# A sparse-attention and mixture block on one Trainium2 core: zero fills on VectorE, later constants behind stage one, and all of batch 0's stage one ahead of the projection weights

## The chip, the cores and the metric

The kernel runs on one core of one Trainium2 chip. The metric is the device time of one execution in microseconds; lower is better. Before the change it is 478.81 us, the median of three runs (478.75, 478.81 and 481.27).

## What is computed

Inputs are q, k and v of 4 batches, 8 heads, 576 positions and 64 columns, and the weights of two blocks. Three steps follow one another:

```python
# stage one: attention with fixed masks; half the heads see the last 32 positions,
# half see every 32nd position before their own
mask_local = (rel >= 0) & (rel < stride)
mask_strided = (rel >= 0) & (pos[None, :] % stride == pos[:, None] % stride)
x = softmax(where(mask, scale * q @ k.T, -1e9)) @ v          # as (4, 576, 512)
# stage two: 4 experts of causal attention, each row takes the 2 of the largest gate
topk = np.argpartition(-(x @ w_gate), K, axis=-1)[..., :K]
out += mask * w * (softmax(causal(scale * q @ k.T)) @ v @ wo[e])
# stage three: h = relu(x @ w_in), a convolution of width 3 over positions, a gate
return (h * sigmoid(conv(h)) @ w_out).astype(np.float32)
```

w_in, conv_w and w_out come as 64-bit words, which the kernel turns into pairs of 32-bit parts on the chip.

## The kernel before

**Stage one** of a batch consists of four units: `s1_local(b, 0)`, `s1_local(b, 1)`, `s1_strided(b, 0)` and `s1_strided(b, 1)`. A unit loads its q and k into a buffer `un` (two exist), lays the mask into PSUM with a matmul of `m_sel` and a mask tile (line 222), adds the scores (line 226), copies them out on ScalarE into `sp` (local) or `pp` (strided), and runs the softmax (lines 229 to 243): maximum on VectorE, subtraction on GpSimd, exponential on ScalarE, sum and reciprocal on VectorE, product on GpSimd. VectorE transposes the result into `lp` (lines 309, 382), ScalarE and GpSimd spread it into the block-diagonal tile `bd` (line 249), and TensorE multiplies with v: `av` for local units (line 324), `avs` for strided ones (line 392). ScalarE and VectorE write the result as two half-precision parts `xt` (lines 252, 254). `sp`, `pp`, `bd`, `vn` and `vs` exist once each, so a unit follows another through them. `bd` must be zero outside its blocks; it is filled once at the start, as are the masks.

**Weights.** `w_proj(kk)`, four times, loads a block of the projection weights into a staging buffer `st` and splits it in two parts (`wvg` on ScalarE, `wqk` and the lower parts on VectorE, lines 722 to 725). `w_wp(hf, kk)`, eight times, loads a block of w_in into an `st` buffer, turns it into numbers (`f64_parts`, lines 697 to 705, over ScalarE, VectorE and GpSimd, with a scratch tile `fc`), and multiplies it with `wo` on TensorE: `wps` (line 750). There are two `st` buffers for all of these blocks. `w_wo` loads `woT`, `w_taps` the taps of the convolution, and `w_out_part` (called O below, tile `ow`) w_out, after the staging buffers have been released.

**Stage two** projects x: `p_v` (`psv`, lines 108 to 110 through line 425) and `p_qk` (`psq`), then per block of rows the attention unit `a_unit` with scores `asc`, mask `m_c`, probabilities `pn` (four zero-filled buffers) and result `zav`, written to `z` or, for the last rows, `zL`. The gate in `p_gate` uses the small constant `tri`. **Stage three** is `s3_step`: `hps`, taps on VectorE (line 637), and `o`.

**What sets the order.** Every piece is a generator; a string of letters (line 823) says in which order they are started and how many steps all live ones take after each: S for a stage-one unit, J for `w_proj`, W for the other weights, P for a projection, A for an attention unit, O and M as above. The framework then schedules what has been emitted, engine by engine, by a timeline of its own, so the rows of an engine do not stand in the order of the code. Each engine executes its own row in order. All loads are issued by SyncE's queue, also in order.

Of the kernel before, what the change touches and what calls it, by code (L numbers as in the profile page):

```python
# [7 lines left out]
F32 = mybir.dt.float32  # L8
F32R = mybir.dt.float32r
U32 = mybir.dt.uint32  # L10
F16 = mybir.dt.float16
BF16 = mybir.dt.bfloat16
ACTF = mybir.ActivationFunctionType
ALU = mybir.AluOpType
# [15 lines left out]
C2 = SM / (Q_S * Q_S)  # L30
# [7 lines left out]
NEG = -1.0e9  # L38
# [7 lines left out]
def moe_stack_kernel(ctx, tc, qk_in, vloc, vstr, w_p, wo_t, w_in, conv_w, w_out, out):  # L46
    nc = tc.nc
    B, S, _ = vstr.shape
    D = 64
    DM, DFF = w_in.shape  # L50
    E = wo_t.shape[1] // D
    KD = DM // 128
# [10 lines left out]
    const = pool("const", 1)  # L63
# [10 lines left out]
    act, dve, gp = nc.scalar, nc.vector, nc.gpsimd  # L74
# [20 lines left out]
    def copy_a(out, in_, scale=1.0):  # L95
        act.activation(out=out, in_=in_, func=ACTF.Copy, scale=scale)  # L96
# [29 lines left out]
    for rows, nb in ((first, 4), (extra, 1)):  # L126
        for sign in (1, -1):
            gp.affine_select(out=m_sel[rows, 0:nb], in_=m_sel[rows, 0:nb], pattern=[[0, nb], [sign, 32]],
                             compare_op=ALU.is_ge, fill=0.0, base=0, channel_multiplier=-sign)
    gp.affine_select(out=m_loc[first], in_=m_loc[first], pattern=[[0, NG + 1], [1, 64]],  # L130
                     compare_op=ALU.is_gt, fill=NEG / C1, base=0, channel_multiplier=-1)
    gp.affine_select(out=m_loc[first], in_=m_loc[first], pattern=[[0, NG + 1], [-1, 64]],
                     compare_op=ALU.is_ge, fill=NEG / C1, base=32, channel_multiplier=1)
    dve.memset(m_loc[extra, 0], -NEG / C1)
    gp.affine_select(out=m_loc[extra, 0], in_=m_loc[extra, 0], pattern=[[-1, 64]],
                     compare_op=ALU.is_ge, fill=NEG / C1, base=0, channel_multiplier=1)
    gp.affine_select(out=m_loc[extra, 0], in_=m_loc[extra, 0], pattern=[[-1, 64]],
                     compare_op=ALU.is_ge, fill=0.0, base=32, channel_multiplier=1)
    gp.affine_select(out=m_str[first], in_=m_str[first], pattern=[[0, 8], [-1, NPOS]], compare_op=ALU.is_ge,
                     fill=NEG / C1, base=0, channel_multiplier=1)  # L140
    for x in (m_sel, m_loc, m_str):
        dve.tensor_copy(out=x[64:128], in_=x[0:64])
    m_sel = m_sel.rearrange("p j i -> p (j i)")
    m_loc = m_loc.rearrange("p g c -> p (g c)")
    m_str = m_str.rearrange("p n c -> p (n c)")
# [13 lines left out]
    for x in free["vs"] + free["pp"]:  # L159
        dve.memset(x, 0.0)  # L160
    for _, x in free["bd"]:
        gp.memset(x, 0.0)

    def take(what):

# [3 lines left out]

    def give(what, x):  # L170
        free[what].append(x)

    m_c = const.tile([128, S], BF16, name="m_c")
    gp.memset(m_c, 0.0)
    gp.affine_select(out=m_c[:, S - 128:], in_=m_c[:, S - 128:], pattern=[[-1, 128]], compare_op=ALU.is_ge,
                     fill=NEG / C2, base=0, channel_multiplier=1)
    tri = const.tile([128, E, E], F32, name="tri")
    gp.memset(tri, 0.0)
    gp.affine_select(out=tri, in_=tri, pattern=[[1, E], [-1, E]], compare_op=ALU.is_gt,
                     fill=-1.0, base=0, channel_multiplier=0)  # L180
    gp.tensor_scalar(out=tri, in0=tri, scalar1=1.0, scalar2=None, op0=ALU.add)

    pn_free = []

# [495 lines left out]
            "h": pool("h", H_BUFS), "g": pool("g", G_BUFS), "pn": pool("pn", 1)}  # L680
    pn_free.extend(late["pn"].tile([128, 1280], F16, name=f"pn{i}") for i in range(4))
    zL = [late["zl"].tile([128, 2, 4, 66], F32R, name=f"zL{i}") for i in range(2)]
    for x in pn_free:
        gp.memset(x.bitcast(U32), 0)
    for x in zL:
        gp.memset(x.bitcast(F32), 0.0)
    wout = []
    stg = tc.alloc_tile_pool(name="stg", bufs=2)
    woT = stg.tile([128, KD, E * D], F32, tag="woT", bufs=1, name="woT")
# [41 lines left out]
    def w_wo():  # L731
        nc.sync.dma_start(out=woT, in_=wo_t.rearrange("(k p) n -> p k n", p=128))
        yield
# [3 lines left out]
    def w_wp(hf, kk):  # L737
        cs = slice(512 * hf, 512 * hf + 512)
        t = stg.tile([128, 512, 2], U32, tag="st", name="st")
        nc.sync.dma_start(out=t.rearrange("p n w -> p (n w)"), in_=w_in[128 * kk:128 * kk + 128, cs].bitcast(U32))  # L740
        wi = stg.tile([128, 512], F32, tag="wi", name="wi")
        fc = stg.tile([128, 512], F32, tag="fc", name="fc")
        yield
        a, f = f64_parts(t, fc)
        e2("wa").tensor_tensor(out=wi, in0=a, in1=f, op=ALU.add)
        yield
        if kk == 0:
            wps[hf] = [ps_o.tile([128, 512], F32, tag=f"o{r}", name="wps") for r in range(2)]
        for r in range(2):
            nc.tensor.matmul(out=wps[hf][r], lhsT=woT[:, kk, 128 * r:128 * r + 128], rhs=wi,  # L750
                             start=kk == 0, stop=kk == KD - 1)
        if kk == KD - 1:
            yield
            for r in range(2):
                copy_a(wp[0][:, r, cs], wps[hf][r])
                sub(dve, wp[1][:, r, cs], wps[hf][r], wp[0][:, r, cs].bitcast(F32))
            if hf == 1:
                done.add("wp")

    def w_taps():  # L760
        t = stg.tile([128, 1024], U32, tag="st", name="ct")[:, 0:2 * 3 * KF].rearrange("p (n w) -> p n w", w=2)
        nc.sync.dma_start(out=t.rearrange("p n w -> p (n w)"), in_=conv_w.bitcast(U32))
        yield
        a, f = f64_parts(t, taps)
        gp.tensor_tensor(out=taps, in0=a, in1=f, op=ALU.add)
        yield
        done.add("taps")
# [11 lines left out]
    def mix(*streams):  # L779

        at = [(((i + 0.5) / len(s), n, x)) for n, s in enumerate(streams) for i, x in enumerate(s)]
        return [x for _, _, x in sorted(at, key=lambda t: t[:2])]
# [21 lines left out]
    def rel():  # L804
# [8 lines left out]
        "S": [u for b in range(B) for u in s1_items(b)],  # L813
        "J": [w_proj(kk) for kk in range(KD)],
        "P": [u for b in range(B) for u in p_items(b)],
        "W": [w_wo()] + [w_wp(hf, kk) for hf in range(2) for kk in range(KD)] + [w_taps()],
        "A": [u for b in range(B) for u in a_items(b)],
        "O": [w_out_part(f, hf) for f in range(KF) for hf in range(2)],
        "M": [s3_step((b, ch), f) for b in range(B) for ch in range(2) for f in range(0, KF, 2)]
             + [s3_step(None, f) for f in range(0, KF, 2)],  # L820
    }
    streams = {k: iter(v) for k, v in streams.items()}
    order = list("SSJJJJSS") + mix("W" * 10, "P" * 13, "S" * 4) + ["R"]
    for b in range(B):
        m = "M" * (KF // 2 if b else 0)
        o = "O" * (8 if b == 0 else 0)
# [66 lines left out]
```

## Time and profile before

| | |
|---|---|
| profiled execution, its own time | 479.27 us |
| span of its trace | 477.6 us |
| median of three runs | 478.81 us |
| mean granted TensorE clock, share of full speed | 0.953 |
| TensorE matmuls busy | 407.0 us, 85% |
| VectorE busy | 343.6 us, 72% |
| ScalarE busy | 312.3 us, 65% |
| GpSimd busy | 182.5 us, 38% |

The trace is one execution. Times in its rows count from the start of the span. A row of the timeline gives the start, the time from first start to last end, the engine, the line, the operation, the tile written and those read (without buffer numbers), shape and type, how many instructions are merged in it, and in brackets the idle time of the engine before it with what ended it. A row of the windows gives start and end, length, the busy time of PE, PEld (its weight loads), DVE, ACT and POOL with their instructions, the granted clock, the busy share of the DMA engines and GB/s. A row of the waits says which engine and operation waited for which, for how long in total, how often, and the longest. PE is TensorE, DVE VectorE, ACT ScalarE, POOL GpSimd, SPq SyncE's queue of loads and stores. Several matmuls overlap, so a sum of their single durations is more than their busy time.

### The profile page before, as it was taken

The numbers are of one execution on the slowest core, as the hardware profiler recorded it, in microseconds if no ns is written. First come the engines' busy times: TensorE is split into PE (matmuls) and PEld (weight loads), VectorE is DVE, ScalarE is ACT, GpSimd is POOL, SyncE is SP. The second block draws the span as 40 slices with busy tenths as digits, with TensorE's granted clock in tenths as the row PEclk, the third lists the DMA queues.
The fourth block names the chain that finished last, engine by engine and source line by source line (L and its number), as shares of the span: only waits on it lengthen the run. The fifth ranks groups of instructions, "written<-read, shape, count | busy, mean of one in ns | idle before, by whom it ended". The sixth has DMA issues, their size and how long they took to land.

```text
span 477.6 us, 12531 instructions
## 1 busy us (share of the span) xinstructions
PE 407.0 (85%) x4736; PEld 296.3 (62%) x4736; DVE 343.6 (72%) x970; ACT 312.3 (65%) x833; POOL 182.5 (38%) x247
## 2 busy tenths in 40 slices
PE   0565869797677589999999899999999999999994
PEld 0352446565545467667777667767876677778873
DVE  4498776879979988987874795588757887465651
ACT  1172453568868747777982796698568997567662
POOL 8156656334654532643530243123212333233231
PEclk9995889999579879999999999999999999999999
DMA  5985574236695762253723044254313655101011
GB/s 151 262 266 163 117 224 133 73 112 134 130 181 153 178 140 73 55 112 75 133 44 71 1 102 82 23 117 86 60 51 56 104 104 99 45 1 44 1 46 44
DMA packets 105981, 48.31 MB, mean 101 GB/s; under 512 B 77504, under 2 KB 100032, under 8 KB 105920
## 3 DMA queue, kind: packets, MB, share of 16 engines
q1 hardware_dynamic: 105920, 47.50, 43.0%
q8 instruction: 37, 0.61, 0.5%
q14 instruction: 24, 0.20, 0.1%
HBM read 27.56 MB, written 4.72 MB: 68 GB/s over the span
## 4 chain that ended last, share of the span: by engine, by line
PE 52%; DVE 18%; DMA 13%; issue 5%; ACT 5%; SPq 4%; POOL 2%; POOLq 0%; ACTq 0%; DVEq 0%
PE o L109 7%; PE o L108 7%; PE o L110 6%; DMA st<-in_dram 5%; DMA apt<-pn 4%; PE zav L585 4%; PE asc L535 4%; PE hps L108 4%; DMA ow<-in_dram 3%; PE hps L109 3%; PE hps L110 2%; PE psq L108 2%; PE psq L110 2%; PE psq L109 2%; PE psv L108 2%
## 5 line engine op out<-in xcount | busy, mean ns | idle before, releaser
L637 DVE SCALAR_TENSOR_TENSOR t<-hs,taps,t 128x256 f32<-128x256 f32 x144 | 78.5, 548 | 33.1 <-ACT t L96 32.0
L105 POOL TENSOR_TENSOR gl<-t,gh 128x512 fp32r<-128x512 f32 x36 | 48.3, 1341 | 73.5 <-ACT gh L96 49.5
L109 PE MATMUL o<-wout,gl 128*128 128x512 f32 x144 | 59.1, 410 | 2.3 <-POOL gl L105 2.3
L110 PE MATMUL o<-wout,gh 128*128 128x512 f32 x144 | 56.7, 394 | 0.0
L108 PE MATMUL o<-wout,gh 128*128 128x512 f32 x144 | 55.2, 416 | 0.6 <-ACT gh L96 0.4
L105 POOL TENSOR_TENSOR pn<-apf,pn 64x64 f16<-64x64 f32 (+4 forms) x40 | 33.7, 846 | 51.7 <-ACT pn L96 38.9
L545 ACT ACTIVATE apf<-apf,anm 64x64 f32<-64x64 f32 (+4 forms) x80 | 44.6, 559 | 6.1 <-DVE anm L539 5.7
L585 PE MATMUL zav<-apt,v 128*64 128x128 f16 (+2 forms) x720 | 35.7, 224 | 11.1 <-DMA apt<-pn 4.6
L108 PE MATMUL hps<-z,wp 128*128 128x258 f32 x128 | 40.7, 318 | 2.4 <-ACT hs L100 2.2
L585 PEld LDWEIGHTS <-v 128*64 128x64 f16 (+1 forms) x720 | 24.7, 109 | 26.4 <-issue 16.7
L100 ACT ACTIVATE hs<-hps 128x257 f32<-128x257 f32 (+2 forms) x72 | 27.5, 383 | 20.0 <-PE hps L110 19.6
L108 PE MATMUL psq<-xt,wqk 128*128 128x288 f16 x128 | 37.5, 293 | 2.0 <-DVE v L431 0.9
L96 ACT ACTIVATE t<-hs,taps 128x256 f32<-128x256 f32 x72 | 36.4, 509 | 3.0 <-POOL gl L105 0.7
L539 DVE CUSTOM_DVE_ANT_0 apf<-asc,m_c 64x64 f32<-64x64 f32 (+4 forms) x80 | 32.8, 423 | 7.6 <-PE asc L535 6.4
L110 PE MATMUL psq<-xt,wqk 128*128 128x288 f16 x128 | 37.2, 291 | 0.0
L109 PE MATMUL psq<-xt,wqk 128*128 128x288 f16 x128 | 37.2, 291 | 0.0
L109 PE MATMUL hps<-z,wp 128*128 128x258 f32 x128 | 36.5, 285 | 0.0
L110 PE MATMUL hps<-z,wp 128*128 128x258 f32 x128 | 36.3, 284 | 0.0
L109 PEld LDWEIGHTS o<-wout,gl 128*128 128x128 f32 x144 | 27.0, 188 | 10.4 <-POOL gl L105 4.2
L108 PE MATMUL psv<-wvg,xt 128*128 128x260 f16 (+1 forms) x80 | 24.6, 308 | 9.5 <-DVE xt L254 6.7
L535 PE MATMUL asc<-qk,qk 64*128 64x288 f16 (+4 forms) x192 | 30.6, 283 | 0.0
L110 PEld LDWEIGHTS o<-wout,gh 128*128 128x128 f32 x144 | 27.1, 188 | 5.0 <-issue 0.2
(165 smaller groups left out, 1070.0 us busy)
## 6 DMA issues: line engine op xcount, KB each, us to landing
ow<-in_dram SPq DMA_DIRECT2D x16, 256.0 KB
st<-in_dram SPq DMA_DIRECT2D x8, 512.0 KB
out_dram<-ob SPq DMA_DIRECT2D x16, 256.0 KB
un<-in_dram SPq DMA_DIRECT2D x16, 252.0 KB
vs<-in_dram SPq DMA_DIRECT2D x32, 72.0 KB
vn<-in_dram SPq DMA_DIRECT2D x16, 128.0 KB
un<-in_dram SPq DMA_DIRECT2D x8, 240.0 KB
st<-in_dram SPq DMA_DIRECT2D x4, 386.0 KB
```

Of the source, the lines that this page charges most:

```text
L96: act.activation(out=out, in_=in_, func=ACTF.Copy, scale=scale)
L100: act.activation(out=out, in_=in_, func=ACTF.Relu)
L105: eng.tensor_tensor(out=out, in0=a, in1=b, op=ALU.subtract)
L108: nc.tensor.matmul(out=out, lhsT=ah, rhs=bh, start=first, stop=False)
L109: nc.tensor.matmul(out=out, lhsT=al, rhs=bh, start=False, stop=False)
L110: nc.tensor.matmul(out=out, lhsT=ah, rhs=bl, start=False, stop=last)
L535: nc.tensor.matmul(out=scs[par], lhsT=qk[a][p0:p0 + 64, 0, q0:q0 + rows], rhs=qk[l][p0:p0 + 64, 1, c0:c0 + cw], start=n == 0, stop=n == 2)
L539: dve.tensor_tensor_reduce(out=pfs[par][:, c0:c0 + cw], in0=scs[par], in1=m_c[:rows, S - w + c0 if rows == 128 else S - 128:][:, :cw], sca ...
L545: act.activation(out=pfs[par], in_=pfs[par], func=ACTF.Exp, scale=-1.0, bias=nm[:, par, len(cuts) - 1:len(cuts)], accum_out=den[:, par:par ...
L585: nc.tensor.matmul(out=av[64 * par:64 * par + 64, 0:rows], lhsT=v2[a][:kk, kb, D * e:D * e + D], rhs=pts[par][:kk, l, kb], start=(kb == 0 ...
L637: dve.scalar_tensor_tensor(out=tv, in0=taps_at[i][k], scalar=w, in1=tv, op0=ALU.mult, op1=ALU.add)
```

## The change

All that is not named here is the same code.

1. The copies of the three masks to the upper 64 partitions move from VectorE to ScalarE.
2. `bd` is filled by VectorE instead of GpSimd.
3. `m_c`, `tri`, `pn` and `zL` are made in a new piece `w_init`, the first of the stream W; their fills, and the last step of `tri`, are on VectorE, their selections stay on GpSimd.
4. The string of letters begins with all four stage-one units of batch 0, then W (which is `w_init`), then the four projection blocks. Before, two units, the four blocks and the other two units came in this order.
5. Line numbers move: what stands at line 226 before is at 216, 254 at 244, 724 at 727, 750 at 753, 740 at 743.

```diff
--- before.py
+++ after.py
@@ -139,7 +139,7 @@
     gp.affine_select(out=m_str[first], in_=m_str[first], pattern=[[0, 8], [-1, NPOS]], compare_op=ALU.is_ge,
                      fill=NEG / C1, base=0, channel_multiplier=1)
     for x in (m_sel, m_loc, m_str):
-        dve.tensor_copy(out=x[64:128], in_=x[0:64])
+        copy_a(x[64:128], x[0:64])
     m_sel = m_sel.rearrange("p j i -> p (j i)")
     m_loc = m_loc.rearrange("p g c -> p (g c)")
     m_str = m_str.rearrange("p n c -> p (n c)")
@@ -159,7 +159,7 @@
     for x in free["vs"] + free["pp"]:
         dve.memset(x, 0.0)
     for _, x in free["bd"]:
-        gp.memset(x, 0.0)
+        dve.memset(x, 0.0)
 
     def take(what):
 
@@ -169,16 +169,6 @@
 
     def give(what, x):
         free[what].append(x)
-
-    m_c = const.tile([128, S], BF16, name="m_c")
-    gp.memset(m_c, 0.0)
-    gp.affine_select(out=m_c[:, S - 128:], in_=m_c[:, S - 128:], pattern=[[-1, 128]], compare_op=ALU.is_ge,
-                     fill=NEG / C2, base=0, channel_multiplier=1)
-    tri = const.tile([128, E, E], F32, name="tri")
-    gp.memset(tri, 0.0)
-    gp.affine_select(out=tri, in_=tri, pattern=[[1, E], [-1, E]], compare_op=ALU.is_gt,
-                     fill=-1.0, base=0, channel_multiplier=0)
-    gp.tensor_scalar(out=tri, in0=tri, scalar1=1.0, scalar2=None, op0=ALU.add)
 
     pn_free = []
 
@@ -680,10 +670,23 @@
             "h": pool("h", H_BUFS), "g": pool("g", G_BUFS), "pn": pool("pn", 1)}
     pn_free.extend(late["pn"].tile([128, 1280], F16, name=f"pn{i}") for i in range(4))
     zL = [late["zl"].tile([128, 2, 4, 66], F32R, name=f"zL{i}") for i in range(2)]
-    for x in pn_free:
-        gp.memset(x.bitcast(U32), 0)
-    for x in zL:
-        gp.memset(x.bitcast(F32), 0.0)
+    m_c = const.tile([128, S], BF16, name="m_c")
+    tri = const.tile([128, E, E], F32, name="tri")
+
+    def w_init():
+
+        yield
+        dve.memset(m_c.bitcast(U32), 0)
+        gp.affine_select(out=m_c[:, S - 128:], in_=m_c[:, S - 128:], pattern=[[-1, 128]], compare_op=ALU.is_ge,
+                         fill=NEG / C2, base=0, channel_multiplier=1)
+        dve.memset(tri, 0.0)
+        gp.affine_select(out=tri, in_=tri, pattern=[[1, E], [-1, E]], compare_op=ALU.is_gt,
+                         fill=-1.0, base=0, channel_multiplier=0)
+        dve.tensor_scalar(out=tri, in0=tri, scalar1=1.0, scalar2=None, op0=ALU.add)
+        for x in pn_free:
+            dve.memset(x.bitcast(U32), 0)
+        for x in zL:
+            dve.memset(x.bitcast(F32), 0.0)
     wout = []
     stg = tc.alloc_tile_pool(name="stg", bufs=2)
     woT = stg.tile([128, KD, E * D], F32, tag="woT", bufs=1, name="woT")
@@ -813,14 +816,14 @@
         "S": [u for b in range(B) for u in s1_items(b)],
         "J": [w_proj(kk) for kk in range(KD)],
         "P": [u for b in range(B) for u in p_items(b)],
-        "W": [w_wo()] + [w_wp(hf, kk) for hf in range(2) for kk in range(KD)] + [w_taps()],
+        "W": [w_init(), w_wo()] + [w_wp(hf, kk) for hf in range(2) for kk in range(KD)] + [w_taps()],
         "A": [u for b in range(B) for u in a_items(b)],
         "O": [w_out_part(f, hf) for f in range(KF) for hf in range(2)],
         "M": [s3_step((b, ch), f) for b in range(B) for ch in range(2) for f in range(0, KF, 2)]
              + [s3_step(None, f) for f in range(0, KF, 2)],
     }
     streams = {k: iter(v) for k, v in streams.items()}
-    order = list("SSJJJJSS") + mix("W" * 10, "P" * 13, "S" * 4) + ["R"]
+    order = list("SSSSWJJJJ") + mix("W" * 10, "P" * 13, "S" * 4) + ["R"]
     for b in range(B):
         m = "M" * (KF // 2 if b else 0)
         o = "O" * (8 if b == 0 else 0)
```

SyncE's queue, from the end of the second local unit's q and k (`un_117`) on. `st` with 772 columns is a projection block, `vs` the strided v, `un_116` here the strided q and k. Before:

```order
L264 DMA un_117<-in_dram 128x96
L718 DMA st<-in_dram 128x772 x2
L372 DMA vs_120<-in_dram 18x8x128 x4
L732 DMA woT<-in_dram 128x4x256
L351 DMA un_116<-in_dram 128x4x126 x2
L718 DMA st<-in_dram 128x772
L355 DMA un_116<-in_dram 128x2x72
L718 DMA st<-in_dram 128x772
```

SyncE's queue now, from the same load on:

```order
L254 DMA un_117<-in_dram 128x96
L362 DMA vs_120<-in_dram 18x8x128
L341 DMA un_116<-in_dram 128x4x126 x2
L345 DMA un_116<-in_dram 128x2x72
L362 DMA vs_120<-in_dram 18x8x128 x3
L721 DMA st<-in_dram 128x772 x2
L735 DMA woT<-in_dram 128x4x256
```

The projection blocks have moved behind `vs` and the strided q and k.

VectorE, from the maximum of the first local unit (`nm`) to the transpose into `lp`. Before (two projection blocks are split in front of these rows):

```order
L232 TENSOR_REDUCE nm<-sp_121 128x10
L238 TENSOR_REDUCE den<-sp_121 128x10
L239 TENSOR_SCALAR den<-den 128x10
L240 RECIPROCAL den<-den 128x10
L93 TENSOR_SCALAR wqk_139<-st 128x512
L724 SCALAR_TENSOR_TENSOR wvg_142<-st,wvg_141 128x260
L724 SCALAR_TENSOR_TENSOR wqk_140<-st,wqk_139 128x512
L309 STREAM_TRANSPOSE lp_123<-sp_121 128x640
```

VectorE now, from the same maximum to the same transpose:

```order
L222 TENSOR_REDUCE nm<-sp_121 128x10
L228 TENSOR_REDUCE den<-sp_121 128x10
L229 TENSOR_SCALAR den<-den 128x10
L230 RECIPROCAL den<-den 128x10
L93 TENSOR_SCALAR wqk_128<-st 128x512
L727 SCALAR_TENSOR_TENSOR wvg_131<-st,wvg_130 128x260
L727 SCALAR_TENSOR_TENSOR wqk_129<-st,wqk_128 128x512
L222 TENSOR_REDUCE nms<-pp_122 128x16
L299 STREAM_TRANSPOSE lp_123<-sp_121 128x640
```

The first maximum stands in front of all projection blocks; the first block and the maximum of the strided unit (`nms`) stand between it and the transpose.

TensorE, up to the first projection of batch 0 (`psv`). `avs` is the last product of batch 0's stage one, `wps` a product of w_in; `scs` belongs to batch 1. Before:

```order
L750 MATMUL wps<-wi,woT 128x512 x2
L226 MATMUL sc<-un_117 32x64 x2
L750 MATMUL wps<-wi,woT 128x512 x2
L222 LDWEIGHTS m_sel
L222 MATMUL scs<-m_str,m_sel 128x144
L226 MATMUL scs<-un_116 18x18 x12
L392 MATMUL avs<-bd_124,vs_120 64x72 x16
L226 MATMUL scs<-un_116 18x18 x20
L108 LDWEIGHTS xt_188
L108 MATMUL psv<-wvg_141,xt_188 128x260
```

TensorE now, up to the same first projection:

```order
L212 MATMUL scs<-m_str,m_sel 128x144
L216 MATMUL scs<-un_117 18x18 x31
L382 MATMUL avs<-bd_124,vs_120 64x72 x16
L216 MATMUL scs<-un_117 18x18
L753 MATMUL wps<-wi,woT 128x512 x2
L212 LDWEIGHTS m_sel
L212 MATMUL scs<-m_str,m_sel 128x144
L216 MATMUL scs<-un_116 18x18 x11
L108 LDWEIGHTS xt_173
L108 MATMUL psv<-wvg_130,xt_173 128x260
```

Of the products of w_in, the one in front of the first projection now follows the last `avs`; it is the third of eight, where four stood in front before.

## Rows read from the trace of the kernel before

**Rows 1.** Busy time by stretch: us, engines' busy us, granted clock, DMA share, GB/s.

```profile
0.00:67.79 67.79, 35.26 (x781) 23.48 (x782) 45.16 (x87) 24.66 (x53) 37.66 (x58) 0.90 0.72 198
67.79:100.70 32.91, 30.13 (x399) 20.04 (x398) 26.42 (x66) 17.20 (x45) 17.10 (x21) 0.95 0.41 109
100.70:200.00 99.30, 78.62 (x1198) 56.02 (x1198) 84.77 (x278) 72.29 (x218) 44.96 (x59) 0.86 0.59 135
200.00:440.00 240.00, 232.51 (x2213) 173.31 (x2212) 171.74 (x510) 178.40 (x481) 73.08 (x96) 1.00 0.35 70
```

**Rows 2.** Waits of TensorE, 0 to 110 us: total, times, longest.

```profile
PE sc L222 <- POOL m_loc L137: 10.9, 1, 10.9
PE wps L750 <- POOL wi L745: 5.8, 1, 5.8
PE scs L226 <- DMA un<-in_dram: 3.9, 2, 3.4
PE psv L108 <- DVE xt L254: 3.7, 1, 3.7
```

**Rows 3.** Timeline of GpSimd and VectorE, first 11 us.

```profile
0.80 2.23 POOL L162 MEMSET bd<- 128x2560 f32 x1 [0.29 <-POOLq L880]
...
5.69 1.76 POOL L684 MEMSET pn<- 128x640 uint32 x3
...
1.49 0.91 DVE L160 MEMSET vs<- 128x1024 f32 x1 [0.16 <-issue]
...
3.06 0.11 DVE L134 MEMSET m_loc<- 32x64 bf16 x1
...
5.77 2.70 DVE L142 COPY m_str<-m_str 64x144 bf16<-64x144 bf16 x1 [2.60 <-POOL m_str L139]
```

**Rows 4.** Timeline of ScalarE, VectorE, GpSimd, TensorE: stage one of batch 0.

```profile
15.58 0.42 ACT L96 ACTIVATE wvg<-st 128x260 f16<-128x260 f32 x1 [13.49 <-DMA st<-in_dram]
...
16.38 0.68 DVE L724 SCALAR_TENSOR_TENSOR wqk<-st,wqk 128x512 f16<-128x512 f32 x1
...
17.53 0.75 ACT L96 ACTIVATE sp<-sc 128x320 f32<-128x320 f32 x2
...
22.99 1.26 POOL L242 TENSOR_TENSOR sp<-sp,den 128x640 f32<-128x640 f32 x1 [2.23 <-DVE den L240]
...
25.64 0.84 DVE L309 STREAM_TRANSPOSE lp<-sp 128x640 f32<-128x640 f32 x1
...
30.55 3.46 PE L324 MATMUL av<-bd,vn 128*64 128x128 f32 x32
...
46.59 2.19 PE L392 MATMUL avs<-bd,vs 128*64 128x72 f32 x32
...
55.24 1.97 PE L324 MATMUL av<-bd,vn 128*64 128x128 f32 x32 [2.35 <-POOL bd L91]
```

**Rows 5.** Loads of the page (KB each), and 40 equal slices of 11 to 30 us.

```profile
un<-in_dram SPq DMA_DIRECT2D x16, 252.0 KB
...
vs<-in_dram SPq DMA_DIRECT2D x32, 72.0 KB
...
GB/s 226 320 174 72 129 318 312 380 346 282 221 194 190 186 163 159 144 188 277 346 320 347 352 362 366 355 367 360 364 346 340 351 264 217 249 242 375 397 326 258
```

**Rows 6.** w_in: its eight loads (first and last start), and two of its products.

```profile
L740 SPq DMA_DIRECT2D st<-in_dram x8: 328/355/529, 25.8 to 78.6; - x8
...
57.79 1.98 PE L750 MATMUL wps<-wi,woT 128*128 128x512 f32 x4
...
93.95 1.98 PE L750 MATMUL wps<-wi,woT 128*128 128x512 f32 x4
```

**Rows 7.** Timeline of TensorE: first projection, first scores of attention.

```profile
67.79 0.38 PE L108 MATMUL psv<-wvg,xt 128*128 128x260 f16 x1 [3.71 <-DVE xt L254]
...
100.72 0.22 PE L535 MATMUL asc<-qk 64*64 64x64 f16 x2
```

**Rows 8.** One VectorE step of w_in's blocks: ns minimum, median, maximum.

```profile
L699 DVE TENSOR_SCALAR fc<-fc x8: 364/426/1348, 34.8 to 85.2; 128x512 uint32<-128x512 uint32 x8
```

## The prediction

> **What bounds the kernel now.** I read the windows first [rows 1]. From 200 to 440 us TensorE is busy 232.5 of 240 us: no idle time is left there worth naming. From 100.7 to 200 it is busy 78.6 of 99.3 us while VectorE has 84.8, so that stretch is paced by VectorE, and no instruction of it is added or removed. The first 67.79 us hold only 35.3 us of TensorE work: 32.5 us are idle, the largest piece of idle time in the program. From 67.79, where the projections of batch 0 start, to 100.7, where its first attention scores stand, TensorE is busy 30.1 of 32.9 us.
>
> Then I read who it waited for in the first part [rows 2]: 10.9 us for the last mask, 5.8 us for the operand of w_in's first product, 3.9 us for the strided q and k, 3.7 us for the last split of stage one. So the length of the program hangs on how early stage one of batch 0 is finished, as long as nothing later is late by itself. Everything up to the first attention score is the same work in both kernels; the program becomes shorter by the idle time that is taken out of it.
>
> **The masks.** Before, GpSimd has fills between its selections [rows 3]: 2.23 us for bd, 1.76 for three of the four pn, and those of m_c, tri, zL and the fourth pn. They go to VectorE, which does 1024 elements in 0.91 us; bd's 2560 are then an estimated 2.3 us, pn and zL together 3.2 us. VectorE has little else there, and one copy of its own that takes 2.70 us beside GpSimd's fills leaves it. The one instruction on the path that now stands behind bd is the fill of m_loc's extra rows: before it stands at 3.06, now 2.3 us for bd and some 0.4 for m_c and tri come ahead, so it ends near 5.9; two short selections of GpSimd follow, and the copy to the upper half is ScalarE's. First scores at about 6.8 instead of 10.95.
>
> **These 4 us are worth nothing by themselves.** Before, the eviction of the first scores waits on ScalarE behind two casts of projection weights, to 17.53; the softmax is done at 24.25 and its transpose starts at 25.64, also behind weight splits [rows 4]. Now evictions start near 9 and, with the same 6.7 us of chain, the softmax ends near 16. But on VectorE the transpose stands behind the split of the first weight block. That block is now issued behind vs (four loads of 72 KB) and the strided q and k (two of 252 KB and a small one), 0.81 MB and a little more; at the 180 GB/s that the slices show from 16 to 20 us, while such loads run [rows 5], these are 4.5 us and a little, so it lands near 15.58 + 4.9 = 20.5. Its splits (15.58 to 17.06 before, 1.5 us) and one reduction later the transpose starts near 22.5, and the first product av at about 25 instead of 30.55. The slack between 16 and 22.5 hides the masks' gain as well as anything that VectorE's fills might cost.
>
> **The strided half and the rest of stage one.** The strided scores have their q and k near 18, and their product avs stood at 46.59 because their transpose and copies queued behind the first w_in words. Going through the new order by hand with the durations of before: the third and fourth weight blocks land near 28 and 32 (the second pair waits for the two staging buffers), the second softmax is normalised at 35, the copies end at 36, avs starts at 36: 10.6 us earlier. The second local unit's copies follow the first w_in block on GpSimd, av near 46 instead of 55.24.
>
> **What is given back: w_in.** All twelve weight blocks go through two staging buffers, in the order projections, then w_in. The first w_in load is issued when the third projection block is split: before at 25.8 [rows 6], now at about 32.3 (landing 28, VectorE's queue with the two ow blocks in front to 30.7, 1.5 us of splits). So w_in is 6.5 us late at its start. Its first product comes at about 44. In TensorE's new order three such products stand in front of the first projection; and on VectorE the last split of stage one stands behind pieces of the third and fourth w_in blocks. Third block issued when GpSimd has finished with the first (44), landed at 48, split by 53, its GpSimd steps to 55.8; fourth issued at 51.3, landed 55.4, split by 59.2; then the last two splits of x, with one reduction between, end near 61. **First projection at 61** instead of 67.79 [rows 7].
>
> Bounds on this step. Early end: if the splits of x do not meet the fourth w_in block, 56.5, right after the last avs. Late end: if the third product comes as long after the first w_in load as before (57.79 - 25.8 = 32.0), it starts at 64.3, and the projections at 66.3. I take 61, about midway, where the walk ends.
>
> **From there to attention.** 32.9 us before; one more pair of w_in products falls into it (four matmuls, 1.98 us) and 33 small score products fewer (an estimated 0.4 us, at the pace of 64x18 ones): 34.5 us. Scores of attention at 61 + 34.5 = 95.5 instead of 100.7: 5.2 us earlier. Behind them both kernels do the same; the order on each engine is identical in the last third, and in between only neighbours change places, which I put at plus or minus 2.
>
> **Sum.** The profiled execution took 479.27 us (span 477.6), 0.46 over the median of 478.81. 479.27 - 5.2 - 0.46 = **473.6 us** on the median's footing.
>
> **A rule weighed.** VectorE's single-input operations of 512 elements took 0.43 us in the median and up to 1.35 us, the longest beside a GpSimd operation [rows 8]. The Trainium skill, "SBUF — State Buffer", section "Who interferes with whom", says that such an operation in a two-port mode and a GpSimd operation exclude each other, the later one standing for the whole of the earlier. The trace agrees, and this speaks against the change, as it packs VectorE's and GpSimd's work of 22 to 60 us more closely: if four more of the operations that lead to the last split were held 0.9 us each, the projections would start at 64.6 and the time be 477.2.
>
> **Rivals.**
> - *w_in paces it, the gain is lost.* If the last w_in product, now right in front of the last two projections, starts between 93 and 98 (before 93.95), attention's scores come 5.0 us later (2.0 for four products, 3.0 for 24 projections), at 98 to 103: within 0.5% of before, about 479. For it: the two buffers' eight loads took from 25.8 to 78.6, steps of 7.5 us. Against: before, these steps shared VectorE with stage one, which is now further ahead. Chance 0.2.
> - *Slower, the same mechanism at its full price.* If every w_in step keeps its old length, the last product comes 6.5 us later, at 100.5, TensorE stands still in front of it, and attention begins at 105.5: 4.8 us late, 483.6. It decides from 98 on. Chance 0.15.
> - *Bytes, not order.* 13.4 MB are moved up to 67.79 (198 GB/s); if their sum set the start, the order of loads would bring nothing: 478.8. Against it stands that the DMA engines were busy 0.72 of that stretch only. The Trainium skill, "SBUF — State Buffer", section "A bandwidth-pool intuition that's wrong (but worth ruling out)", calls HBM almost always the end-to-end bottleneck; the trace does not bear that out here. Chance 0.04.
> - *More.* Stage one does not meet the fourth w_in block: projections at 56.5, and the stalls of the 32.9 us go too (2.8): attention at 88.2, 12.5 us earlier, 466.3. Chance 0.14.
> - *Not what it says.* The first q and k land only when the masks were ready before: the slack of 6.5 us to the transpose covers this, so it costs nothing.
>
> **How the numbers follow.** Forecast (3 to 9 us gained) 0.47, more 0.14, lost 0.2, slower 0.15, bytes 0.04. The range reaches from near the "more" case, 467.5, to 481.5, which leaves out about 0.07 below and 0.13 above; the forecast's own is 470 to 476. A measurement of this kernel tells 0.5% (2.4 us) from no change: faster takes the forecast and "more" (0.61), same the lost gain and the bytes with a little of the rest (0.23), slower 0.16.
>
> **What would show it.** Right: first scores near 7 with ScalarE's eviction near 9, transpose near 22, avs near 36, the first w_in load near 32, projections at 58 to 64, attention's scores at 92 to 98, and windows from there on of the old lengths. Wrong: a wait of several us in front of the w_in products or the last projections, or a stretch from attention to 200 us that is longer than 99.3 us by more than 2.

## The result and the profile after

The changed kernel takes 475.33 us in the median (473.02 to 479.78), the kernel before, beside it, 480.38 us. The ratio is **0.9897, 95% interval [0.9873, 0.9921]**: about 5 us faster, as forecast. A ratio compares fast runs of a kernel with fast runs of the kernel before taken beside them, so it need not be the quotient of two medians. The profiled execution after has a span of 473.7 us at a granted clock of 0.946 (477.6 and 0.953 before).

The number came out. The reasons, as the experiments show, mostly did not: some 4 of the 5 us were made behind attention's start, where I had expected nothing.

Windows of the changed kernel, cut at its own first projection and first attention scores, as [rows 1] were cut before. The columns are the stretch and its length, busy us of TensorE, its weight loads, VectorE, ScalarE, GpSimd (with instruction counts), the granted clock, the DMA share and GB/s:

```profile
0.00:65.18 65.18, 36.30 (x865) 23.72 (x866) 46.45 (x90) 26.14 (x58) 31.86 (x50) 0.84 0.75 206
65.18:98.76 33.58, 28.34 (x327) 19.09 (x316) 26.55 (x69) 16.46 (x43) 14.87 (x19) 1.00 0.40 110
```

The first projection moved by 2.6 us only (67.79 before), attention's scores by 2.0 (100.72 before). The last copy of outputs out of PSUM (`ob`, on ScalarE; called the last copy below) starts 3.9 us earlier (467.9, before 471.8). So in this pair of profiles half of the gain lies behind attention's start.

The start of stage one went as walked. The timeline of the changed kernel, first 36 us, with ScalarE's eviction (the copy of the scores out of PSUM), VectorE's fill of bd, its fill of m_loc and its transpose, and TensorE's first scores and products, which answer [rows 3, 4]:

```profile
7.38 0.42 PE L212 MATMUL sc<-m_loc,m_sel 64*128 64x320 bf16 x1 [7.38 <-POOL m_loc L137]
...
25.99 1.33 PE L314 MATMUL av<-bd,vn 128*64 128x128 f32 x10
...
10.66 0.77 ACT L96 ACTIVATE sp<-sc 128x320 f32<-128x320 f32 x2 [2.83 <-PE sc L216]
...
3.70 2.19 DVE L162 MEMSET bd<- 128x2560 f32 x1 [0.60 <-issue]
...
6.29 0.11 DVE L134 MEMSET m_loc<- 32x64 bf16 x1
...
21.05 0.83 DVE L299 STREAM_TRANSPOSE lp<-sp 128x640 f32<-128x640 f32 x1
...
35.47 1.22 PE L382 MATMUL avs<-bd,vs 128*64 128x72 f32 x32 [2.45 <-POOL bd L91]
```

Strided `avs` stands at 35.47 (before 46.59): 11.1 us earlier, as predicted. Of these 11.1 us 2.6 are left at the first projection. Where they went is seen on ScalarE. Its timeline in the changed kernel, the first step of the w_in blocks (`fc<-st`) and what is queued behind it; in brackets how long ScalarE stood idle before the row, and for what:

```profile
36.26 0.67 ACT L700 ACTIVATE fc<-st 128x512 f32<-128x512 f32 x1 [4.34 <-DMA st<-in_dram]
...
49.73 0.67 ACT L700 ACTIVATE fc<-st 128x512 f32<-128x512 f32 x1 [4.73 <-DMA st<-in_dram]
...
56.85 0.66 ACT L700 ACTIVATE fc<-st 128x512 f32<-128x512 f32 x1 [3.96 <-DMA st<-in_dram]
57.41 0.65 ACT L96 ACTIVATE st<-st 128x512 f32<-128x512 uint32 x1
57.97 0.28 ACT L96 ACTIVATE pp<-scs 128x144 f32<-128x144 f32 x1
```

ScalarE takes its instructions in order. From 52.9 to 56.85 it stands in front of a w_in block that has not landed, and the copy `pp` of the next batch's strided scores, for which TensorE waits, stands behind. TensorE's timeline of the same stretch shows the price:

```profile
58.29 0.28 PE L212 MATMUL scs<-m_str,m_sel 64*128 64x144 bf16 x1 [2.40 <-ACT pp L96]
58.50 0.74 PE L216 MATMUL scs<-un 64*18 64x18 f32 x62
59.30 2.19 PE L382 MATMUL avs<-bd,vs 128*64 128x72 f32 x32
61.42 0.25 PE L216 MATMUL scs<-un 64*18 64x18 f32 x2
61.60 3.23 PE L753 MATMUL wps<-wi,woT 128*128 128x512 f32 x4
64.76 0.23 PE L212 MATMUL scs<-m_str,m_sel 64*128 64x144 bf16 x1
64.92 0.33 PE L216 MATMUL scs<-un 64*18 64x18 f32 x22
65.18 0.28 PE L108 MATMUL psv<-wvg,xt 128*128 128x260 f16 x1
```

The four matmuls of w_in take 3.23 us here and 1.98 in [rows 6]. Windows show TensorE's clock: first the changed kernel from 47.1 us on, in whose second row the granted clock is at the lower of its two levels (0.50, 1.2 of 2.4 GHz), then the kernel before over the same part, at the full one. The fall at 53.9 us came after 4.18 busy us in 6.70:

```profile
47.10:53.80 6.70, 4.18 (x73) 2.88 (x72) 4.17 (x9) 2.69 (x6) 2.33 (x3) 1.00 0.58 169
53.90:64.10 10.20, 7.73 (x138) 4.46 (x138) 5.96 (x12) 4.40 (x10) 6.30 (x7) 0.50 0.69 202
```

```profile
50.80:67.70 16.90, 10.84 (x222) 6.51 (x221) 12.69 (x23) 6.81 (x15) 11.67 (x12) 1.00 0.67 171
```

ScalarE's waits from 26 to 66 us, summed: us in all, times, longest. First the changed kernel, then the kernel before:

```profile
ACT fc L700 <- DMA st<-in_dram: 15.8, 5, 4.7
```

```profile
ACT fc L697 <- DMA st<-in_dram: 5.6, 4, 2.3
```

So what stage one no longer waits for at its front, ScalarE now waits for at w_in's loads: 15.8 us instead of 5.6.

### The profile page after: what moved, and what is told of

Same layout as the page of the kernel before. It is cut to its first block, busy times and chain, and to the rows that moved or that the text cites. A ratio compares the mean times of both kernels' runs of the same rounds, so it can differ in the third digit from the quotient of the medians.

```text
span 473.7 us, 12540 instructions
## 1 busy us (share of the span) xinstructions
PE 406.1 (86%) x4736; PEld 295.6 (62%) x4736; DVE 349.8 (74%) x977; ACT 314.3 (66%) x836; POOL 174.1 (37%) x237
## 4 chain that ended last, share of the span: by engine, by line
PE 47%; DVE 20%; DMA 15%; ACT 5%; issue 5%; SPq 5%; POOL 2%; POOLq 0%; ACTq 0%; DVEq 0%
DMA st<-in_dram 7%; PE o L108 6%; PE o L109 6%; PE o L110 5%; PE zav L575 4%; DMA apt<-pn 4%; PE hps L108 3%; DVE apf L529 3%; PE hps L110 3%; DMA ow<-in_dram 3%; PE asc L525 3%; PE hps L109 3%; DVE t L627 2%; PE psq L108 2%; PE psq L110 2%
## 5 line engine op out<-in xcount | busy, mean ns | idle before, releaser
L627 DVE SCALAR_TENSOR_TENSOR t<-hs,taps,t 128x256 f32<-128x256 f32 x144 | 82.1, 573 | 32.9 <-ACT t L96 31.6
L108 PE MATMUL psq<-xt,wqk 128*128 128x288 f16 x128 | 37.8, 296 | 2.9 <-DVE v L421 2.3
L110 PE MATMUL psq<-xt,wqk 128*128 128x288 f16 x128 | 37.7, 295 | 0.0
L109 PE MATMUL psq<-xt,wqk 128*128 128x288 f16 x128 | 37.7, 295 | 0.0
L108 PEld LDWEIGHTS hps<-z,wp 128*128 128x128 f32 x128 | 24.3, 190 | 12.2 <-ACT hs L100 4.9
L558 DVE SCALAR_TENSOR_TENSOR pn<-apf,aden,pn 64x64 f16<-64x64 f32 (+4 forms) x40 | 27.1, 677 | 4.8 <-ACT pn L96 4.5
```

The lines of the kernel that those rows point to most:

```text
L108: nc.tensor.matmul(out=out, lhsT=ah, rhs=bh, start=first, stop=False)
L109: nc.tensor.matmul(out=out, lhsT=al, rhs=bh, start=False, stop=False)
L110: nc.tensor.matmul(out=out, lhsT=ah, rhs=bl, start=False, stop=last)
L558: dve.scalar_tensor_tensor(out=pn[:, 1, :w], in0=pfs[par], scalar=den[:, par:par + 1], in1=pn[:, 0, :w], op0=ALU.mult, op1=ALU.subtract)
L627: dve.scalar_tensor_tensor(out=tv, in0=taps_at[i][k], scalar=w, in1=tv, op0=ALU.mult, op1=ALU.add)
```

## The experiments

After the result I held two pairs of theories against each other. On the parts: A, the order of the items carries the gain; B, the fills carry it. On what sets attention's start: C, the loop of w_in's blocks through two staging buffers; D, the last split of stage one. By "the order of the items" I mean point 4 of the change (the string of letters), by "the fills" points 1 to 3. Every kernel below but those held in the later order was compiled as it is, so its scheduler also chose an order of its own behind attention.

**The order alone** (`e_order`): the kernel before with the four stage-one units first.

```diff
-    order = list("SSJJJJSS") + mix("W" * 10, "P" * 13, "S" * 4) + ["R"]
+    order = list("SSSSJJJJ") + mix("W" * 10, "P" * 13, "S" * 4) + ["R"]
```

> The kernel before with the order of the change alone: four stage-one units of batch 0, then the projection blocks; all fills and copies stay where they were. Theory A (order carries the gain; the masks' 4 us lie in the slack before the first weight split): masks at 10.9, first softmax normalised near 20.7, transpose near 21.5, time within 0.3% of the changed kernel, ratio to before 0.987 to 0.993. Theory B (the fills carry it): ratio 0.998 to 1.003, transpose still near 25.

Measured: 485.3 us, ratio 1.0128 [1.0079, 1.0177]: slower. The last w_in load starts at 85.3 us (78.6 in [rows 6]), attention at 105.5, as TensorE's timeline of this kernel has it:

```profile
102.23 1.88 PE L750 MATMUL wps<-wi,woT 128*128 128x512 f32 x4
...
105.51 0.22 PE L535 MATMUL asc<-qk 64*64 64x64 f16 x2
```

Theory A falls. Nor does the order alone bring stage one forward: its first strided product `avs` stands at 45.83 (46.59 before, 35.47 with the whole change):

```profile
45.83 2.19 PE L392 MATMUL avs<-bd,vs 128*64 128x72 f32 x32
```

**The fills alone** (`e_fills`): the changed kernel with the old order of the items.

```diff
-    order = list("SSSSWJJJJ") + mix("W" * 10, "P" * 13, "S" * 4) + ["R"]
+    order = list("SSJJJJSSW") + mix("W" * 10, "P" * 13, "S" * 4) + ["R"]
```

> The changed kernel with the old order of starts (two units, four projection blocks, two units, then the new constants); the fills and copies stay changed. Theory A: masks near 7, but the eviction of the first scores again behind the casts at 15 to 17, ratio to before 0.997 to 1.003. Theory B: ratio 0.987 to 0.993.

Measured: 481.87 us, ratio 1.0054 [1.0019, 1.009]: slower, though attention starts at 98.2. From there to the last copy 374.1 us pass, where the changed kernel takes 369.2 and the kernel before 371.1. Theory B falls too: as they were compiled, neither part alone carries the gain. The fills alone do bring the strided product forward, by 5.9 us:

```profile
40.65 2.19 PE L382 MATMUL avs<-bd,vs 128*64 128x72 f32 x32
```

**A third staging buffer** in the changed kernel (`a_st3`) and in the kernel before (`b_st3`), at the three places that take an `st` tile:

```diff
-        t = stg.tile([128, 512, 2], U32, tag="st", name="st")
+        t = stg.tile([128, 512, 2], U32, tag="st", name="st", bufs=3)
```

> The changed kernel with three staging buffers for weight blocks instead of two. Theory C (w_in's eight loads through two buffers set the start of attention, 22 us behind the last load in both kernels): last w_in load some 8 to 12 us earlier, attention's scores 3 to 6 us earlier, at 92 to 96, ratio to before 0.977 to 0.985. Theory D (the last split of stage one sets it): attention's scores stay within 1 us of 98.8, ratio 0.988 to 0.992.

> The kernel before with three staging buffers. Theory C: last w_in load 8 us earlier than 78.6, but the first projection now sets attention, 33 us behind 67.8: scores 0 to 3 us earlier than 100.7, ratio 0.993 to 1.0, and the gap to the changed kernel with three buffers grows to 1.2 to 2%. Theory D: ratio 0.998 to 1.002, gap unchanged at 1%.

Measured: `a_st3` 478.3 us, ratio 0.9985 [0.9955, 1.0015]; `b_st3` 472.54 us, 0.9828 [0.9767, 0.9889]. Neither C nor D had the time of either: `a_st3` starts attention where C had put it and gains nothing, `b_st3` starts it at 99.2, w_in's last load at 70.0, and gains 1.7%. In `a_st3` ScalarE's wait for w_in's loads is nearly gone, and attention starts at 95.1. ScalarE's waits of this kernel, 26 to 66 us:

```profile
ACT fc L700 <- DMA st<-in_dram: 1.1, 2, 0.8
```

Yet the time is that of the kernel before: from attention to the last copy 376.6 us pass. Six kernels, whose instructions behind attention are the same but for a few steps of w_out, take from 368.5 (`b_st3`) to 376.6 us there. So the start of attention did not tell the time, and what lies behind it had to be held fixed.

**The later order held.** The built programs show that the scheduler gives each kernel another order of the same instructions behind attention's start, on all five engines. The traces show how far: between the kernel before and the changed one, some 150 of VectorE's 820 instructions there stand more than three places from where they stood, up to 22, and on TensorE whole groups of matmuls up to 110 places. From the first emitted instruction that is the same in all kernels, their names agree. So I read the order of one kernel's instructions behind its first `asc` on each engine (some 2,980 on TensorE, 720 on VectorE, 650 on ScalarE) and chained them in another kernel by ordering edges that carry no wait:

```diff
     with tile.TileContext(nc, schedule_with_timeline_sim=True) as tc:
         moe_stack_kernel(tc, *args)
+        made = {i.name: i for i in nc.cur_bb.bb.instructions}
+        late = [[f"I-{x}" for x in seq.split()] for seq in LATE.values()]
+        for seq in late:
+            for first, second in zip(seq, seq[1:]):
+                tc.add_manual_dep(made[second], first, mybir.DependencyInfo(
+                    mybir.DependencyClass.NoSync, mybir.DependencyReason.DATA), reason="later order")
...
+LATE = {
+    "PE": """1436 1437 ...
```

`LATE` is the table of names. What stands in front of `asc` stays as each kernel has it, but for steps of w_out that the held order puts behind it: one on VectorE in `h_a_lb`, some ten on three engines in `h_b3_la` below. The traces have the orders that were meant, in front of `asc` and behind it. What the edges cost by themselves (a kernel held in its own order) was not run.

`h_a_lb` is the changed kernel up to attention, and behind it the order of the kernel before; `h_b_la` the reverse.

> The changed kernel up to attention's first product, and behind it, on all five engines, the order of the kernel before (held by ordering edges without a wait). In the profiles so far attention starts at 100.72 us before and 98.76 after, and from there to the last output copy 371.1 us pass before and 369.2 after; the scheduler had put the later instructions in another order. Theory X (the shift passes through: the end is the start of attention plus a length that belongs to the later order): start 98.8, length 371.1, last copy near 469.9, 2.0 us under before, ratio 0.996. Theory Y (the later stretch gives an earlier start back): start 98.8, last copy 471.8, ratio 1.000. Theory Z (the whole gain comes with the early part, the later order has no share in it): ratio 0.990.

> The kernel before up to attention's first product, and behind it, on all five engines, the order of the changed kernel (held by ordering edges without a wait). Theory X (end = start of attention + a length that belongs to the later order): start 100.7, length 369.2, last copy near 469.9, ratio 0.996. Theory Z (the later order has no share in the gain): start 100.7, length 371.1, ratio 1.000. If the whole gain lay in the later order: length 366, ratio 0.990.

Measured: `h_a_lb` 478.73 us, ratio 0.9983 [0.9948, 1.0017]; `h_b_la` 475.92 us, ratio 0.9921 [0.9885, 0.9957]. With the changed kernel's 0.9897 these are the four corners:

| up to attention | order behind it: before's | order behind it: the changed kernel's |
|---|---|---|
| before | 1 | 0.9921 |
| changed | 0.9983 | 0.9897 |

The later order is worth 0.8% (1 - 0.9921, plus or minus 0.36%) and 0.9% (0.9983 - 0.9897, 0.42%): about 4 us. The early part is worth 0.2% both times (0.34% and 0.43%), about 1 us, which is not told from nothing. Theory Z (the whole gain in the early part) falls. X's even split, 0.996 twice, lies within the first interval and just outside the second; the whole gain in the later order, 0.990 for `h_b_la`, lies within.

Windows of `h_b_la`, then of the kernel before, from the first `asc` to the first copy of outputs, and from there to the last:

```profile
98.46:227.95 129.49, 113.72 (x1614) 79.66 (x1614) 110.92 (x339) 96.61 (x274) 57.81 (x72) 0.84 0.55 124
227.95:466.83 238.88, 231.36 (x1946) 174.85 (x1943) 165.12 (x480) 173.94 (x461) 69.56 (x97) 1.00 0.29 62
```

```profile
100.72:232.27 131.55, 110.87 (x1641) 79.04 (x1640) 111.05 (x349) 97.16 (x284) 58.93 (x73) 0.90 0.57 124
232.27:471.78 239.51, 230.12 (x1916) 173.57 (x1915) 160.99 (x471) 172.09 (x452) 68.81 (x96) 1.00 0.29 60
```

In the new order some 30 more matmuls are left for the last stretch, and it is not longer for them; TensorE stands idle for 15.8 us in the stretch before (129.49 - 113.72) instead of 20.7, at a lower clock. TensorE's waits from 100 to 230 us, the kernel before (here several wait on VectorE's attention reductions `anm` and `den`), then `h_b_la`:

```profile
PE zav L585 <- DVE xt L254: 4.1, 2, 3.4
PE psv L108 <- DVE xt L254: 3.0, 2, 2.6
PE avs L392 <- DVE qk L484: 2.2, 1, 2.2
PE asc L535 <- DVE anm L539: 1.6, 2, 0.9
PE zav L585 <- DVE den L240: 1.3, 1, 1.3
...
PE scs L222 <- DVE anm L539: 1.1, 1, 1.1
```

```profile
PE zav L585 <- DVE xt L254: 4.1, 2, 3.7
PE avs L392 <- DVE qk L484: 2.1, 1, 2.1
PE psv L108 <- DVE xt L254: 2.1, 1, 2.1
PE hps L108 <- ACT z L96: 1.7, 1, 1.7
PE psv L108 <- DVE z L105: 1.6, 1, 1.6
```

The large waits are the same; those on `anm` and `den` are nearly gone, and about as many us on `z` have come. So these lists do not say where the gain lies, and which change of place makes it was not taken apart.

**The early part under one later order.** The other six hold the order of the changed kernel behind attention: its early part with a third buffer (`h_a3_la`), the fills alone (`h_ef_la`), the kernel before with a third buffer (`h_b3_la`), the order of items alone (`h_eo_la`), and the last two with a third buffer (`h_ef3_la`, `h_eo3_la`). Their edits are those above. The expectation of `h_a3_la` says that 374.1 us pass behind attention in the changed kernel with three buffers; that is the figure of `e_fills`, and `a_st3` took 376.6. In the expectations of the last four, C and D are named anew: C, stage one's chain and w_in's end at about the same time and either alone brings little; D, w_in's alone sets the start.

> The changed kernel with three staging buffers instead of two for the weights up to attention's first product (by itself: attention at 95.06, but 374.1 us from there to the last copy, ratio 0.9985), and behind it the order of the changed kernel. Theory X (shift passes through): start 95.1, length 369.2, last copy near 464.3, 7.5 us under before, ratio 0.984. Theory Y (an earlier start is given back later, by a clock or a load that runs on its own time): as the changed kernel or worse, ratio 0.990 to 0.998, with a length of 373 or more.

> The fills moved alone, the old order of the items (stage one in two halves around the projections' weights; by itself: attention at 98.17, 374.1 us from there to the last copy, ratio 1.005), and behind attention's first product the order of the changed kernel. Theory X (the loss of the fills alone lay in the later order that came with it): start 98.2, length 369.2, last copy near 467.4, 4.4 us under before, ratio 0.991, as the changed kernel. Theory Y (the early part itself makes the later stretch longer, as by the clock or the state of the weights): length 372 to 374, ratio 1.000 to 1.005.

> The kernel before with a third staging buffer for the weights, and behind attention's first product the order of the changed kernel. Beside it stand, with the same later order: the kernel before 0.992, the changed kernel 0.990, the changed kernel with three buffers 0.979. Theory C (two chains of about one length end where attention starts: stage one's, which the change shortens, and that of w_in's eight blocks through two buffers, which it does not; either alone brings little): start 99, ratio 0.990. Theory D (w_in's chain alone sets the start, the third buffer does it all, whatever the front): start 94 to 95, ratio 0.979 to 0.981.

> The new order of the items alone, the fills as before, and behind attention's first product the order of the changed kernel (by itself, with the later order that came with it, ratio 1.013, attention at 105.5). If its loss comes from the early part (w_in's last block loaded at 85.3 instead of 78.6 us): start 104 to 105.5, 5 us over the kernel before with this later order, ratio 1.002 to 1.005. If it came with the later order: start 100, ratio 0.992.

> The fills moved, the old order of the items, a third staging buffer, and behind attention's first product the order of the changed kernel. Theory C with the fills as the part that shortens stage one's chain: start 92 to 95, ratio 0.976 to 0.981, as the changed kernel with three buffers (0.979). If the new order of the items carries that: start 98, ratio 0.986, as with two buffers.

> The new order of the items, the fills as before, a third staging buffer, and behind attention's first product the order of the changed kernel. Theory C: the third buffer takes back what the order costs w_in's chain, and stage one's start is as late as before: start 98 to 99, ratio 0.988 to 0.991. If the order itself shortens stage one's chain: start 94 to 95, ratio 0.980.

Measured, with the first `asc` of the profiled execution, and the us from there to the last copy:

| early part | two buffers: us, ratio | `asc`, rest | three buffers: us, ratio | `asc`, rest |
|---|---|---|---|---|
| as before | 475.92, 0.9921 [0.9885, 0.9957] | 98.5, 368.4 | 471.18, 0.9833 [0.9791, 0.9874] | 96.8, 364.3 |
| order of items | 480.16, 1.0014 [0.9989, 1.004] | 104.7, 367.7 | 472.48, 0.9854 [0.9815, 0.9893] | 98.5, 368.7 |
| fills | 473.34, 0.9865 [0.9824, 0.9906] | 99.3, 369.3 | 472.58, 0.9852 [0.9819, 0.9885] | 98.9, 367.7 |
| both (the change) | 475.33, 0.9897 [0.9873, 0.9921] | 98.8, 369.2 | 469.71, 0.9789 [0.9747, 0.9832] | 92.4, 367.4 |

What follows:

- *The shift passes through, roughly.* With the later order held the rest is 364.3 to 369.3 us over a start that varies by 12 us. Theory X holds at its ends (`h_eo_la`, `h_a3_la`); in between, single profiles are too coarse (below).
- *The order of the items costs, with two buffers:* 0.9% alone (1.0014 - 0.9921, plus or minus 0.44%); on top of the fills 0.3%, not told from nothing. Its early part starts attention 6 us late; the 1.1% that `e_order` lost beyond that (1.0128 - 1.0014) came with its own later order.
- *The fills bring* 0.6% by themselves (0.9921 - 0.9865, plus or minus 0.55%), at the edge of what can be told, and 1.2% on top of the order of the items (1.0014 - 0.9897, 0.35%), which is clear. So the early part of the change comes to little because the order's loss and the fills' gain meet in it. The fills' loss in `e_fills` came with the later order: 1.0054 against 0.9865.
- *The third buffer* brings 1.1% to the changed kernel, 0.9% to the kernel before, 1.6% to the order alone, and nothing that can be told to the fills alone (0.1%). I had expected 0.990 (two chains, either of which suffices) or 0.980 (w_in's alone) of `h_b3_la`; its interval leaves out the first and takes in the second, but its start, 96.8, lies between 94 to 95 and 99. That the loop through two buffers paces the start is shown for the order of the items, where the loop is longest: there the third buffer starts attention 6.2 us earlier. It is not so for the fills alone: w_in's last load moves from 81.2 to 65.4 us, attention from 99.3 to 98.9. There another chain sets the start, as C in its pure form had it.
- *What sets the start with three buffers* is not shown by a run, but the traces point at stage one: w_in's last product stands at 80.9 to 85.8 us in all four kernels, 11 to 15 us ahead of attention, while the last strided product of batch 0 stands at 53.2 in `h_a3_la` and at 63.0 to 65.4 in the other three.
- `h_a3_la` is faster than both kernels, 469.71 us. Its ratio is told from that of `h_ef3_la` and `h_eo3_la` (0.9852, 0.9854, against 0.9789: 0.6%, plus or minus 0.54% and 0.58%) only just, and from that of `h_b3_la` (0.9833) not at all. Why stage one ends early only with order and fills together stays open.

Windows of `h_a3_la` up to its first projection and to its first `asc`:

```profile
0.00:61.13 61.13, 36.47 (x780) 24.90 (x781) 48.08 (x92) 28.02 (x60) 32.02 (x49) 0.86 0.82 226
61.13:92.36 31.23, 30.75 (x401) 20.24 (x399) 25.73 (x64) 14.29 (x40) 14.77 (x18) 0.95 0.28 83
```

With w_in's loop loosened the projections start at 61.1, where the walk of the prediction had put them with two buffers. ScalarE's wait for w_in's loads is 3.0 us in this kernel from 26 to 66 us.

## Why the prediction was right, and where it was wrong

**The masks** went as predicted: first scores at 7.38 (6.8), the eviction at 10.66 (near 9), bd's fill 2.19 us (2.3). The fills ended at 10.3, before VectorE's first maximum at 11.46, and cost nothing, as said.

**"These 4 us are worth nothing by themselves": this step failed.** I had put all of stage one's gain down to the order of the items. The strided `avs` stands at 45.83 with the order alone, at 40.65 with the fills alone and at 35.47 with both, and with the later order held the fills bring 0.6% by themselves and 1.2% on top of the order, which by itself costs 0.9%.

**The transpose and the strided half**: 21.05 (22.5), av 25.99 (25), avs 35.47 (36), first w_in load 31.28 (32.3), first product 44.31 (44), av of the second local unit 47.88 (46). All within 2 us.

**First projection at 61: this step failed.** It came at 65.18, near the late bound of 66.3, and at 67.56 in `h_a_lb`, whose program is the same up to there. The walk had the last two splits of x as the last thing; they were done at 62.9 (the second starts at 62.41 and takes 0.45). What came late stood on other engines: ScalarE's copy behind the fourth w_in block, TensorE's 2.40 us behind that copy, and then the third w_in product in front of the projection, 3.23 us at a granted clock of 0.60, where the late bound had 2.0 us from rows at the full clock. I had followed w_in's blocks on VectorE and GpSimd and not on ScalarE, whose queue holds both w_in's first step and stage one's evictions.

**From there to attention**: 33.6 us (34.5), near. I had counted 33 score products fewer in this stretch; TensorE's trace has 88 fewer (107, before 195), which at the same pace makes 33.8 instead of 34.5. Attention's scores then at 98.76 instead of 95.5.

**"Behind them both kernels do the same", plus or minus 2: this step failed, and it decided the case.** The order behind attention is worth about 4 us between these two kernels, and 1.9% between the fills' own and the changed kernel's. Nor is it only neighbours that change places: instructions of VectorE move by up to 22 places and matmuls by up to 110, and near 400 us, in the last third, some 50 matmuls change places.

So the sum came near by luck, through two errors of opposite sign: the early part gave 1 us instead of 5.2, the later order 4 instead of 0. The rival **w_in paces it, the gain is lost** (attention at 98 to 103, about 479 us) is what the early part did: `h_a_lb` takes 478.73 us, and the third buffer, which loosens w_in's loop, brings the changed kernel 1.1%. Its full price, **slower** (last w_in product 100.5, attention 105.5, 483.6 us), is met by the order alone: 102.2, 105.5 and 485.3 us. I gave the two 0.35 together; what made the forecast come out was not among the cases at all.

**Bytes, not order** falls: in `h_a3_la` as many bytes (13.8 MB, 13.4 in the changed kernel) move at 226 GB/s to the first projection, with the DMA engines 0.82 busy, instead of 206 and 0.75.

**The rule on shared ports** would have put the projections at 64.6. They came at 65.18, but not by it: the operation that was to be held takes 0.43 us in the median and at most 1.15, before 0.43 and 1.35 [rows 8], and the three single-input steps of this kind (lines 701, 702 and 706; 698, 699 and 703 before) take 15.9 us in all up to attention, before 19.4. The changed kernel's row (ns minimum, median, maximum):

```profile
L702 DVE TENSOR_SCALAR fc<-fc x8: 384/428/1148, 37.4 to 84.7; 128x512 uint32<-128x512 uint32 x8
```

The Trainium skill, "SBUF — State Buffer", section "Who interferes with whom", has such operations shut each other out. Neither figure shows more of it after the fills moved than before.

## What to carry to other kernels

Where a scheduler orders the whole program, an edit at its front also makes another program behind it: hold the later order fixed before a gain of 1% is put down to the edit. Follow a moved load on every engine that works on it, the one that merely copies too, and look at what is queued behind its first step. A loop through two buffers in front of a bound stretch can give back what is won ahead of it; here loosening it brought 1.1% on top of the change.

## What the runs showed of the hardware that was not expected

- Two programs that are the same up to attention do not start it at the same time: the kernel before at 100.72 us and `h_b_la` at 98.46, the changed kernel at 98.76 and `h_a_lb` at 99.94. Their first projections differ as well: 67.79 and 67.24, 65.18 and 67.56. One profile each cannot tell 2 us here, and the forecast of 5.2 us rested on one. Twenty executions of the kernel before ran from 477.21 to 484.57 us.
- Four matmuls of w_in take 1.98 us where the granted clock is 1.00 [rows 6], and 3.34 and 3.23 us in the changed kernel (from 44.31 and 61.60), at granted clocks of 0.59 and 0.60: a mix of the two levels, mostly the lower. The kernel before has such stretches too: its first four take 3.78 us (from 41.52). There the clock was at the lower level from 37.1 to 50.8 us and from 67.8 to 71.1; in the changed kernel from 36.9 to 47.0, after 9.23 busy us of TensorE in the 12.8 before, and from 53.9 to 64.1.
- VectorE filled 2560 elements a partition in 2.19 us and 1024 in 0.91; GpSimd had taken 2.23 for the same 2560 [rows 3]. The fills were no faster on VectorE; they only stood elsewhere.
